# Three transpose groups a stretch instead of four, and the weight maximum moved to the head of the stretch

## The chip, the cores and the metric

The kernel runs on one core of a Trainium2 chip. The metric is device time in microseconds of one execution, compared with the kernel before on the same chip. The core has a matmul engine (TensorE, PE in the profile), a vector engine (VectorE, DVE), a scalar engine (ScalarE, ACT), a general engine (GpSimd, POOL) and a queue that issues transfers (SyncE, SP). Each works through its own instructions in order and waits for the others by semaphores. PE writes to PSUM, a small memory of eight banks; DVE and ACT read the results from there.

## What is computed

The reference is sigmoid attention, a Fourier mixing of its output, and a two-layer network, cut here to what matters:

```python
scores = scale * np.matmul(q, k.transpose(0, 1, 3, 2)) - np.log(S)
attn = 1.0 / (1.0 + np.exp(-scores))
x = np.matmul(attn, v)                    # (8, 12, 448, 64) -> (8, 448, 768)
mixed = np.real(np.fft.fft(np.fft.fft(x, axis=1), axis=2))
u = x + mixed
un = (u - mean(u)) / np.sqrt(var(u) + 1e-06)
out = u + np.maximum(un @ w_ch1, 0.0) @ w_ch2
```

There are 8 batches of 448 tokens, 12 heads of 64, a model width of 768 and a hidden width of 3072.

## The kernel before, in words

**Stages.** The program has three parts. In the first (0 to about 460 us of the profile) attention and mixing run for all eight batches. In the second, two blocks of 512 tokens go through the network with plain matmuls, while the weights are split into f16 pairs and stored. In the third (from about 950 us) the other five blocks use a fast product scheme; PE lines 790 and 841 are all of its chain.

**The attention loop.** The loop at line 518 takes two steps t, t+1 at a time; I call one pass a stretch and name it by its even t. There are 192 steps, 24 to a batch. In each stretch the code first empties three lists of work left over by the stretch before (`sp_next`, `act_next`, `dve_next`, lines 519 to 521: transfers, ACT copies, DVE additions). Then come two score blocks (`scores`, line 132: twelve matmuls on PE, two sigmoids on ACT, tile `a`), then two value blocks (`values`, line 152: eight matmuls on PE into `av`). Every second stretch, those with t a multiple of 4, finishes a head pair, and DVE copies `av` to `xT` (line 161). Then `mix_some` issues some mixing on PE. Last come the extras: POOL rounds q and k (`cast`, `qh` and `kh`, line 117), DVE makes the remainders (`rest`, `ql` and `kl`, line 122, also in the stretches with t a multiple of 4), POOL and DVE fold `xT` (`eo`, `fd`, `xp`, lines 175 to 181), loads are issued, and two more things happen: `weight_load` brings a piece of the weights (`wr`), and `weight_max` takes its largest magnitude on DVE (`wmax`, line 264). In the later batches DVE also computes the row statistics of finished tokens (`mv`, `un`, `hl`).

**The mixing.** One batch gives 36 units (lines 246 to 250), each with a cost in microseconds that the program's author wrote down: 24 of `stage_d` (0.33; one matmul each into `psd`), four of `stage_s` (0.65; `pss`) and eight of `add_x` (0.31). A unit of `add_x` is a group of three transposes on PE into one PSUM tile `psx` (line 226); the addition that reads the tile (`u`, line 233) goes to `dve_next`, so it stands on DVE at the head of the next stretch. `mix_some` gets a budget of `2 * UNIT_US` a stretch, adds it to what is left, and issues units while the balance is above zero; the last unit may overdraw it. All of `psd`, `pss` and `psx` share one pool of three PSUM tiles (line 91):

```python
ps_m = mix.enter_context(tc.tile_pool(name="ps_m", bufs=3, space=PSUM, side="right"))
```

A tile can be written again when its reader is done: ACT copies `A` (line 198) and `Q` (line 209), DVE operations `sm` and `df` (line 214), or the addition `u`.

**What fixes the order.** `pin()` at the end of each stretch ties every engine's instructions of that stretch to the order in which they were written. So an engine's order is that of the code, stretch after stretch.

**After the loop.** At step 170 `weight_scales` reduces the maxima (`wm`, DVE), has POOL reduce them over the partitions (line 272), and derives the scales; from there on weights are prepared (`prep_w`, lines 398 to 419: ACT, DVE, ACT, DVE). The last batch's units are issued after the loop by `mix_rest(0.65)` (line 616), together with pieces of the first network matmuls and weight steps.

Of the kernel before, what the change touches and what calls it, by code (L numbers as in the profile page):

```python
# [34 lines left out]
NW2 = 3  # L35
LEAD = 4
LNT = 2
UNIT_US = 0.57
MIX_UP = 8
MIX_STEP = 7  # L40

# [17 lines left out]
def spectral_attention_ffn(tc, q, k, v, w1, w2, cd, cs, ident_in, out):  # L59
# [8 lines left out]
    with ExitStack() as top:  # L68
# [19 lines left out]
        if True:  # L88
# [36 lines left out]
            def scores(t):  # L125

                g, c = divmod(t, 4)
                ps = ps_sc.tile([128, 2, 512], F32, tag="sc", name="sc")
                for n, (kn, qn) in enumerate(((0, 0), (0, 1), (1, 0))):
                    for j in range(2):  # L130
                        h = slice(j * D, (j + 1) * D)
                        nc.tensor.matmul(  # L132
                            ps[:CP, j, :SQ], split[g, 1, kn][h, c * CP:(c + 1) * CP], split[g, 0, qn][h],
                            start=(n == 0), stop=(n == 2))
                att[g, c] = a = wk.tile([CP, 2, SQ], F32, tag="a", name="a", bufs=ABUF)
                nc.scalar.activation(  # L136
                    a, ps[:CP, :, :SQ], AF.Sigmoid, bias=-math.log(S), scale=1.0 / math.sqrt(D))
# [3 lines left out]
            def values(t):  # L141
                g, c = divmod(t, 4)
                gg, pr = divmod(g, 2)
                b, r = divmod(gg, NG)
                p = r + 3 * pr
                a, vr = att.pop((g, c)), vrs[gg]
                if c == 0:
                    avp[g] = ps_av.tile([128, 512], F32, tag="av", name="av")
                ps = avp[g]
                for j in range(2):  # L150
                    h = 2 * pr + j
                    nc.tensor.matmul(  # L152
                        ps[j * D:(j + 1) * D, :SQ], vr[:, c, h * D:(h + 1) * D], a[:, j],
                        start=(c == 0), stop=(c == 3))
                if c < 3:
                    return
                if r == 0 and pr == 0:
                    xts[b] = (fx.tile([128, 6, 2, HS], F32, tag="xT", name="xT", bufs=2),
                              fx.tile([128, 2, 2, 2, 3, HM], F32, tag="xp", name="xp"))
                xT = xts[b][0]  # L160
                nc.vector.tensor_scalar(  # L161
                    out=xT[:, p].rearrange("d r k -> d (r k)"), in0=ps[:, :SQ], scalar1=1.0, scalar2=None,
                    op0=ALU.mult)
# [20 lines left out]
            def mix_units(b):  # L184
                xT, xp = xts[b]
                A = fx.tile([HM, 2, 2, 386], F32, tag="A", name="A")
                ps_d, sd, ut = {}, {}, {}

                def stage_d(kp, c, par, p):
                    m = HM - kp  # L190
                    if par == 0 and p == 0:
                        ps_d[c, kp] = ps_m.tile([128, 512], F32, tag="m", name="psd")
                    ps = ps_d[c, kp]
                    nc.tensor.matmul(
                        ps[:HM, par * 193:par * 193 + 193], xp[:, kp ^ c, c, par, p],
                        cd_sb[:, c, par, p], start=(p == 0), stop=(p == 2))
                    if par == 1 and p == 2:
                        act_next.append(lambda: nc.scalar.activation(
                            A[:, kp, c].rearrange("s (i r) -> s r i", r=2),
                            ps[:HM, 0:386].rearrange("s (r i) -> s r i", r=2), AF.Copy))  # L200

                def stage_s(kp, c):
                    m = HM - kp
                    ps = ps_m.tile([128, 512], F32, tag="m", name="pss")
                    nc.tensor.matmul(
                        ps[:m, :385], cs_sb[:, kp, c, :m], A[:, kp, c, :385], start=True, stop=True)
                    if c == 1:
                        sd["Q", kp] = Q = fx.tile([128, 385], F32, tag="Q", name="Q", bufs=2)
                        act_next.append(lambda: nc.scalar.activation(Q[:m], ps[:m, :385], AF.Copy))
                    else:  # L210
                        Q = sd["Q", kp]
                        sd[kp] = [fx.tile([128, 385], F32, tag=n, name=n, bufs=2) for n in ("sm", "df")]
                        for o, op in zip(sd[kp], (ALU.add, ALU.subtract)):
                            dve_next.append(lambda o=o, op=op: nc.vector.tensor_tensor(
                                out=o[:m], in0=ps[:m, :385], in1=Q[:m], op=op))

                def add_x(kp, r, hf):

                    lo, hi = (1, HM - 1) if r and not kp else (0, HM - kp)
                    s, d = sd[kp]  # L220
                    if hf == 0:
                        ut[kp, r] = fx.tile([128, DM], F32, tag="u", name="u", bufs=3)
                    u = ut[kp, r]
                    ps = ps_m.tile([128, 512], F32, tag="m", name="psx")
                    for i in range(3):
                        nc.tensor.transpose(
                            ps[:HM - kp, i * 128:(i + 1) * 128], xT[:, hf * 3 + i, r, kp:HS:2], ident)
                    y = d if hf == r else s
                    m = HM - kp
                    ysl = y[:m, 384:0:-1] if hf else y[:m, 0:384]  # L230

                    def add():
                        nc.vector.tensor_tensor(
                            out=u[:m, hf * 384:hf * 384 + 384], in0=ps[:m, :384], in1=ysl, op=ALU.add)
                        if hf:
                            base = b * S + (0, 113, 225, 336)[2 * r + kp] - lo

                            cut = lo + (hi - lo) // 16 * 16
                            for i, j in ((lo, cut), (cut, hi)):
                                if i < j:  # L240
                                    sp_next.append(lambda i=i, j=j: nc.sync.dma_start(
                                        u_dram[base + i:base + j, :], u[i:j, :]))
                    dve_next.append(add)


                res = [(0.33, lambda kp=kp, c=c, par=par, p=p: stage_d(kp, c, par, p))
                       for kp in range(2) for c in (1, 0) for par in range(2) for p in range(3)]
                res += [(0.65, lambda kp=kp, c=c: stage_s(kp, c)) for kp in range(2) for c in (1, 0)]
                res += [(0.31, lambda kp=kp, r=r, hf=hf: add_x(kp, r, hf))
                        for kp in range(2) for r in range(2) for hf in range(2)]  # L250
                return res

# [9 lines left out]
            def weight_max(n):  # L262
                i, f = divmod(n, NFC)
                nc.vector.tensor_reduce(
                    out=wmax[:, i, f:f + 1], in_=wtile.pop(n)[:, :, 1].bitcast(F32), op=ALU.max, axis=AX.X,
                    apply_absolute_value=True)
# [170 lines left out]
            def flush(todo):  # L437
                now = list(todo)
                todo.clear()
                for fn in now:  # L440
                    fn()
# [38 lines left out]
            when_w = {}  # L480
# [37 lines left out]
            for t in range(0, TQ + LAG + 4, 2):  # L518
                flush(sp_next)
                flush(act_next)  # L520
                flush(dve_next)
                for i in range(t, t + 2):
                    if i < TQ:
                        scores(i)
                for i in range(t - LAG, t - LAG + 2):
                    if 0 <= i < TQ:
                        values(i)
                mix_some(2 * UNIT_US)
                for i in range(t, t + 2):
                    for fn in extra.pop(i, ()):  # L530
                        fn()
                    for n in when_w.get(i - 1, ()):
                        weight_load(n + 2)
                    for n in when_w.get(i, ()):
                        weight_max(n)
                pin()
            assert not extra, sorted(extra)
            att_ctx.close()
# [2 lines left out]
        with ExitStack() as fast, ExitStack() as st, ExitStack() as early:  # L541
# [73 lines left out]
            while units or act_next or dve_next or sp_next:  # L615
# [4 lines left out]
                n = step % MIX_STEP  # L620
# [274 lines left out]
            for c in range(NPLAIN + 1, NCK):  # L895
                t = (c - NPLAIN - 1) * NQ * NU
# [3 lines left out]
            for g in range(NGR):  # L900
                t = g * NU
# [81 lines left out]
```

## Time and profile before

| | us |
|---|---|
| median of 3 runs (lowest to highest) | 1801.37 (1796.43 to 1805.48) |
| the profiled execution: its time | 1796.9 |
| its span, first to last instruction | 1795.1 |
| PE busy in the span | 1671.5 (93%) |
| DVE busy | 1290.0 (72%) |
| ACT busy | 602.4 (34%) |
| POOL busy | 194.3 (11%) |
| mean granted PE clock | 0.977 |

The time is 1.8 us more than the span, for what lies around it. A row of the table of waits reads: engine, what it was about to do, its line, the engine and line that released it, total idle time in us, number of waits, the longest. A row of the timeline reads: start in us, length in us, engine, line, operation, output and inputs, shapes, how many instructions are merged in the row, and in brackets the idle time before it and what ended it. A row of the stretches' table reads: from and to, length, then busy time and number of instructions of PE, of the weight loads (PEld), of DVE, ACT and POOL, the granted clock, the share of the transfer engines in use, and GB/s.

### The profile page before, as it was taken

How to read it: one execution, taken by the hardware profiler on the slowest of the kernel's cores; microseconds unless marked ns; L12 is line 12 of the kernel's file. 1: busy time of each engine (PE TensorE's matmuls, PEld its weight loads, DVE VectorE, ACT ScalarE, POOL GpSimd, SP SyncE). 2: the span in 40 equal slices, each digit the busy share in tenths (PEclk: the TensorE clock that was granted, in tenths of full speed). 3: DMA queues.
4: the chain of work that ended last, by engine and by line, in shares of the span. 5: the costliest groups of instructions: out<-in, count | busy, mean ns of one | idle time of the engine just before them, and what ended most of it. 6: DMA issues, size and time to landing. Idle time of an engine off the chain costs nothing. (4 is left out here: it accounts for less than half of the span.)

```text
span 1795.1 us, 27673 instructions
## 1 busy us (share of the span) xinstructions
PE 1671.5 (93%) x10996; PEld 1070.2 (60%) x10996; DVE 1290.0 (72%) x2481; ACT 602.4 (34%) x767; POOL 194.3 (11%) x220
## 2 busy tenths in 40 slices
PE   8999999987878777999799999999999999999997
PEld 3555555543533333545357777777777777777774
DVE  3545577656777777467755888888888887888668
ACT  4444444434333333123232322333233323233221
POOL 4434444334000000000000000000000000000000
PEclk9999999998988999999999999999999999999999
DMA  7666767654666664587887466656475656566561
GB/s 234 209 213 211 237 208 240 212 177 118 225 211 211 211 211 140 192 307 278 302 288 271 186 247 234 238 214 242 175 277 206 237 199 254 215 229 241 216 227 59
DMA packets 109139, 394.95 MB, mean 220 GB/s; under 512 B 23521, under 2 KB 49362, under 8 KB 93522
## 3 DMA queue, kind: packets, MB, share of 16 engines
q1 hardware_dynamic: 109010, 393.19, 62.2%
q8 instruction: 86, 1.41, 0.3%
q14 instruction: 43, 0.35, 0.1%
HBM read 316.08 MB, written 73.92 MB: 217 GB/s over the span
## 5 line engine op out<-in xcount | busy, mean ns | idle before, releaser
L841 PE MATMUL pso<-ws,H 128*128 128x384 f16 x2520 | 422.6, 326 | 0.9 <-DVE H L796 0.8
L790 PE MATMUL psf<-ut,ws 128*128 128x256 f16 x3780 | 422.1, 273 | 1.1 <-DVE ur L600 1.1
L790 PEld LDWEIGHTS <-ws 128*128 128x128 f16 x3780 | 369.9, 98 | 50.3 <-issue 1.4
L841 PEld LDWEIGHTS <-H 128*128 128x128 f16 x2520 | 246.4, 98 | 155.8 <-DVE H L796 1.1
L136 ACT ACTIVATE a<-sc 112x900 f32<-112x900 f32 x192 | 166.6, 917 | 156.3 <-PE sc L132 156.1
L850 DVE TENSOR_TENSOR acc<-pso,acc 128x384 f32<-128x384 f32 x350 | 181.9, 550 | 19.0 <-PE pso L841 19.0
L579 PE MATMUL po<-w2h,hh 128*128 128x512 f16 (+1 forms) x384 | 133.7, 348 | 55.5 <-ACT hh L567 54.8
L152 PE MATMUL av<-a,vr 112*64 112x450 f32 x768 | 172.9, 573 | 3.7 <-DVE xT L161 3.7
L815 ACT ACTIVATE F<-F 128x1024 f32<-128x1024 f32 x60 | 63.5, 1058 | 332.0 <-DVE F L796 332.0
L796 DVE TENSOR_TENSOR H<-F,H 128x1024 f16<-128x1024 f32 x120 | 129.5, 1087 | 46.8 <-ACT H L825 46.8
L560 PE MATMUL psh<-ut,w1h 128*128 128x512 f16 x504 | 151.1, 382 | 5.0 <-DVE hl L568 5.0
L579 PEld LDWEIGHTS <-hh 128*128 128x128 f16 x768 | 77.5, 103 | 114.7 <-ACT hh L567 66.0
L579 PE MATMUL po<-w2h,hl 128*128 128x512 f16 (+1 forms) x384 | 132.9, 346 | 3.8 <-DVE hl L568 1.5
L796 DVE TENSOR_TENSOR F<-X,psf 128x256 f32<-128x256 f32 x240 | 98.0, 418 | 51.1 <-PE psf L790 48.1
L579 PE MATMUL po<-w2l,hh 128*128 128x512 f16 (+1 forms) x384 | 133.0, 346 | 0.0
L161 DVE TENSOR_SCALAR xT<-av 128x450 f32<-128x450 f32 x48 | 30.1, 626 | 141.8 <-PE av L152 141.8
L825 ACT ACTIVATE H<-F 128x1792 f16<-128x1792 f32 x60 | 101.8, 1697 | 89.0 <-DVE F L796 89.0
L796 DVE TENSOR_TENSOR F<-F 128x256 f32<-128x256 f32 x240 | 91.2, 421 | 17.7 <-ACT F L815 13.7
L568 DVE SCALAR_TENSOR_TENSOR hl<-psh,hh 128x512 f16<-128x512 f32 x48 | 33.2, 691 | 98.2 <-ACT hh L567 98.1
L132 PE MATMUL sc<-qh,kh 64*112 64x450 f32 x384 | 82.1, 423 | 19.7 <-ACT a L136 10.3
L152 PEld LDWEIGHTS av<-a,vr 112*64 112x64 f32 x768 | 47.8, 139 | 82.9 <-issue 68.3
L560 PE MATMUL psh<-ut,w1l 128*128 128x512 f16 x252 | 96.2, 382 | 0.0
(92 smaller groups left out, 1954.2 us busy)
## 6 DMA issues: line engine op xcount, KB each, us to landing
ws<-w_dram SPq DMA_DIRECT2D x120, 1344.0 KB, 5.9
wr<-w_in SPq DMA_DIRECT2D x80, 768.0 KB, 4.7
t_dram<-wt SPq DMA_DIRECT2D x48, 384.0 KB, 2.3
cb<-t_dram SPq DMA_DIRECT2D x24, 768.0 KB, 5.5
spare<-w_in SPq DMA_DIRECT2D x16, 768.0 KB, 4.6
qr<-q_in SPq DMA_DIRECT2D x48, 225.0 KB, 3.8
kr<-k_in SPq DMA_DIRECT2D x48, 224.0 KB, 3.5
vr<-v_in SPq DMA_DIRECT2D x24, 448.0 KB
```

The source lines that it names most:

```text
L132: nc.tensor.matmul(ps[:CP, j, :SQ], split[g, 1, kn][h, c * CP:(c + 1) * CP], split[g, 0, qn][h], start=(n == 0), stop=(n == 2))
L136: nc.scalar.activation(a, ps[:CP, :, :SQ], AF.Sigmoid, bias=-math.log(S), scale=1.0 / math.sqrt(D))
L152: nc.tensor.matmul(ps[j * D:(j + 1) * D, :SQ], vr[:, c, h * D:(h + 1) * D], a[:, j], start=(c == 0), stop=(c == 3))
L560: nc.tensor.matmul(hs[c, f], l[f][:, m], r[:, m], start=(m == n == 0), stop=(m == NCC - 1 and n == 2))
L568: nc.vector.scalar_tensor_tensor(out=hl, in0=ps, scalar=0.0, in1=hh, op0=ALU.max, op1=ALU.subtract)
L579: nc.tensor.matmul(po[n][:, at:at + hi - lo], l[:, cols], r[f][:, lo:hi], start=(f == 0 and m == 0 and at == 0), stop=(f == NFC - 1 and m ...
L790: nc.tensor.matmul(ps[:, :TH], w[:, x, a, m * 128:(m + 1) * 128], ut[y][:, b, m], start=(m == n == 0), stop=(m == n == 2))
L796: nc.vector.tensor_tensor(out=o, in0=x, in1=y, op=op)
L815: nc.scalar.activation(F[:, 0:4], F[:, 0:4], AF.Relu)
L825: nc.scalar.activation(hts[P][:, 0], F[:, 1:8], AF.Copy)
L841: nc.tensor.matmul(ps[:, :384], H[:, x, a, tp * 128:(tp + 1) * 128], w[:, y, b], start=(j == n == 0), stop=(j == 1 and n == 2))
L850: later(0, lambda: nc.vector.tensor_tensor(out=to, in0=ps[:, :384], in1=to, op=ALU.add))
```

## The change

The budget of a stretch rises from 1.14 to 1.20 us, the written cost of a transpose group from 0.31 to 0.42, and `weight_max` moves: what stood at the end of a stretch now stands at the head of the next one, behind the emptied lists and ahead of the scores.

```diff
-UNIT_US = 0.57
+UNIT_US = 0.6
...
-                res += [(0.31, lambda kp=kp, r=r, hf=hf: add_x(kp, r, hf))
+                res += [(0.42, lambda kp=kp, r=r, hf=hf: add_x(kp, r, hf))
                         for kp in range(2) for r in range(2) for hf in range(2)]
...
                 flush(dve_next)
+                for i in range(t - 2, t):
+                    for n in when_w.get(i, ()):
+                        weight_max(n)
                 for i in range(t, t + 2):
                     if i < TQ:
                         scores(i)
...
                     for n in when_w.get(i - 1, ()):
                         weight_load(n + 2)
-                    for n in when_w.get(i, ()):
-                        weight_max(n)
```

What this does to PE's order is seen at the end of the first batch's mixing. PE before, from the last two `pss` to the last transposes (scores left out; one `av` row stands for a stretch, and the x9 of `psx` are three groups of three):

```order
L152 MATMUL av<-a,vr 64x450 x4
L205 MATMUL pss<-A,cs_sb 112x385 x2
...
L152 MATMUL av<-a,vr 64x450 x4
L226 MATMUL psx<-ident,xT 113x128 x9
...
L152 MATMUL av<-a,vr 64x450 x4
L226 MATMUL psx<-ident,xT 113x128 x3
L226 MATMUL psx<-ident,xT 112x128 x9
...
L152 MATMUL av<-a,vr 64x450 x4
L226 MATMUL psx<-ident,xT 112x128 x3
```

These are stretches 44, 46, 48 and 50: two `pss`, then three groups, four groups, one group. The same four stretches of PE in the changed kernel:

```order
L152 MATMUL av<-a,vr 64x450 x4
L205 MATMUL pss<-A,cs_sb 112x385
L226 MATMUL psx<-ident,xT 113x128 x3
...
L152 MATMUL av<-a,vr 64x450 x4
L226 MATMUL psx<-ident,xT 113x128 x9
...
L152 MATMUL av<-a,vr 64x450 x4
L226 MATMUL psx<-ident,xT 112x128 x9
...
L152 MATMUL av<-a,vr 64x450 x4
L226 MATMUL psx<-ident,xT 112x128 x3
```

Now they hold one `pss` and one group, three groups, three groups, one group; one `pss` has moved from stretch 44 to 42. The units of `stage_d` come 8, 3, 4, 4, 3, 2 a stretch where they came 7, 4, 3, 4, 3, 3. The pattern is the same for each of the seven batches that mix inside the loop.

On DVE the same place, as a difference (- before, + the change; `u` are the additions that free the transposes' tiles):

```order
 L214 TENSOR_TENSOR df<-pss,Q 112x385
-L264 TENSOR_REDUCE wmax<-wr 128x1
 L233 TENSOR_TENSOR u<-psx,df 113x384
 L233 TENSOR_TENSOR u<-psx,sm 113x384 x2
-L161 TENSOR_SCALAR xT<-av 128x450
-L122 TENSOR_TENSOR ql<-qr,qh 128x450
-L122 TENSOR_TENSOR kl<-kr,kh 128x448
-L264 TENSOR_REDUCE wmax<-wr 128x1
 L233 TENSOR_TENSOR u<-psx,df 113x384
+L264 TENSOR_REDUCE wmax<-wr 128x1
```

The fourth addition now stands ahead of `xT`, `ql` and `kl` of stretch 48, and the maximum stands behind the additions instead of ahead of them. On SP the store of the rows whose addition moved up goes ahead of four loads of the same stretch (`vr`, `wr`, `kr`, `qr`). POOL's order is unchanged.

## The prediction

> **What bounds the kernel now.** I read the busy time by parts of the span first; the two that the edit acts in are attention up to the reduction of the maxima, and the end of attention:
>
> ```profile
> 0.00:380.00 380.00, 359.10 (x2185) 196.03 (x2187) 216.54 (x357) 172.25 (x215) 163.75 (x194) 0.99 0.69 221
> 380.00:462.00 82.00, 63.12 (x315) 33.01 (x312) 47.34 (x83) 27.56 (x36) 30.14 (x26) 0.85 0.40 118
> ```
>
> Up to 380 us PE is busy 359 of 380 us while DVE, ACT and POOL are near half. What is left of PE's time there is best read from the table of waits. Between 100 and 380 us, PE's whole table, and then the others' longest:
>
> ```profile
> PE psx L226 <- DVE u L233: 13.4, 6, 2.7
> PE sc L132 <- ACT a L136: 0.6, 1, 0.6
> ...
> ACT a L136 <- PE sc L132: 107.0, 55, 5.9
> DVE xT L161 <- PE av L152: 86.5, 30, 6.3
> ```
>
> In 280 us PE stops for two reasons only: six times for an addition that has to free a transpose tile, and once for a sigmoid. ACT and DVE wait for PE instead, again and again. So here PE is the bound, and an idle microsecond of PE is a microsecond of the program. One of the six, from the timeline of stretch 48:
>
> ```profile
> 100.47 1.25 PE L226 MATMUL psx<-ident,xT 128*113 128x128 f32 x9
> 100.59 0.63 DVE L161 TENSOR_SCALAR xT<-av 128x450 f32<-128x450 f32 x1 [2.25 <-PE av L152]
> 101.67 1.40 DVE L122 TENSOR_TENSOR kl<-kr,kh 128x448 fp32r<-128x448 f32 x1
> 102.99 0.94 DVE L264 TENSOR_REDUCE wmax<-wr 128x1 f32<-128x768 f32 x1
> 103.86 1.01 DVE L233 TENSOR_TENSOR u<-psx,df 113x384 f32<-113x384 f32 x2
> 104.45 0.59 PE L226 MATMUL psx<-ident,xT 128*112 128x128 f32 x3 [2.74 <-DVE u L233]
> 105.27 0.37 PE L132 MATMUL sc<-ql,kh 64*112 64x450 f32 x2
> 106.39 1.73 PE L152 MATMUL av<-a,vr 112*64 112x450 f32 x8
> 108.05 0.59 PE L226 MATMUL psx<-ident,xT 128*112 128x128 f32 x3
> ```
>
> Three groups run at 100.47; the fourth finds all three tiles of the pool taken. The first of them is freed by an addition that stands on DVE behind `xT`, `ql`, `kl` and here a weight maximum, so PE sits until 104.45. The other five waits:
>
> ```profile
> 158.81 0.59 PE L226 MATMUL psx<-ident,xT 128*112 128x128 f32 x3 [2.10 <-DVE u L233]
> 212.97 0.59 PE L226 MATMUL psx<-ident,xT 128*112 128x128 f32 x3 [1.88 <-DVE u L233]
> 268.77 0.59 PE L226 MATMUL psx<-ident,xT 128*112 128x128 f32 x3 [2.74 <-DVE u L233]
> 323.16 0.59 PE L226 MATMUL psx<-ident,xT 128*112 128x128 f32 x3 [2.10 <-DVE u L233]
> 377.30 0.59 PE L226 MATMUL psx<-ident,xT 128*112 128x128 f32 x3 [1.88 <-DVE u L233]
> ```
>
> They are longest (2.74) where the maximum stands last before the additions. The seventh batch mixes while no scores are left to run, and does not wait.
>
> **The change part by part.** *No fourth group.* The stretch that held four groups holds three, so the wait for the fourth goes, if the moved groups find free tiles. Each new place, by the rows of the first batch:
>
> ```profile
> 94.61 0.55 DVE L214 TENSOR_TENSOR df<-pss,Q 112x385 f32<-112x385 f32 x1
> 96.22 1.25 PE L226 MATMUL psx<-ident,xT 128*113 128x128 f32 x9
> ```
>
> In the stretch with the first three groups, the third now needs the tile of the one group issued a stretch earlier. Its addition follows `df`: 94.61 + 0.55 + 0.56 = 95.7. A group costs (1.25 - 0.59) / 2 = 0.33 us of PE by the x9 and x3 rows, and one more comes before, so PE asks at 96.22 + 3 x 0.33 = 97.2: 1.5 us to spare. In the next stretch the tiles were freed at the head, two microseconds before use. The last group needs the first addition behind `kl`: 101.67 + 1.40 + 0.56 = 103.6, and PE now arrives at 101.72 (the end of the x9 at 100.47) plus 3.08 (the next stretch's scores and values, 104.97 to 108.05) = 104.8: 1.2 us to spare. So nothing waits at its new place, and the first five waits are worth 2.74 + 2.10 + 1.88 + 2.74 + 2.10 = 11.56 us.
>
> *The sixth wait* is worth nothing, because the end of attention hangs on another chain:
>
> ```profile
> 374.29 0.63 DVE L161 TENSOR_SCALAR xT<-av 128x450 f32<-128x450 f32 x1 [2.25 <-PE av L152]
> 376.70 1.01 DVE L233 TENSOR_TENSOR u<-psx,df 113x384 f32<-113x384 f32 x2
> 379.10 0.19 DVE L270 TENSOR_REDUCE wm<-wmax 128x2 f32<-128x48 f32 x1
> 386.58 0.37 POOL L272 PARTITION_ALL_REDUCE ws<-wm  x1 [10.29 <-issue]
> 389.71 2.85 PE L152 MATMUL av<-a,vr 112*64 112x450 f32 x8 [3.75 <-DVE xT L161]
> 394.24 0.97 POOL L178 TENSOR_TENSOR fd<-eo 128x450 f32<-128x450 f32 x1 [7.30 <-issue]
> 395.93 2.56 PE L194 MATMUL psd<-cd_sb,xp 128*113 128x193 f32 x10 [2.00 <-DVE xp L181]
> ```
>
> DVE's work after `xT` (374.29, before the wait at 375.4) leads to `wm`, POOL's reduction, DVE's `xT` of stretch 172 and PE's values at 389.71. PE reaches that place earlier by 1.88 and waits longer by as much. Bounds: 0 to 1.88. The reduction starts 7.29 us after `wm` is done (379.29), as long as POOL's pause before `fd`, so I take the chain to start at `wm`. One addition fewer stands ahead of `wm`: 0.47 us (1.01 for two that overlap) gained; bounds 0 and 0.47.
>
> *The clock at that place.* After the 3.75 us wait eight value matmuls take 2.85 us; after the 2.74 us wait the next eight take 1.73 (106.39) and the scores ahead of them 0.37: only long waits slow PE, so removing the short ones gives their length and no more. The Trainium skill, "TensorE: Matmul & The Clock Gate", section "HAM oscillation — how this bites in real kernels", asks for no idle gaps over about 3.4 us. By that rule too the sum has no clock term, but the wait at 389.71, grown to 5.1 us, could not be worse than it is.
>
> *Units elsewhere.* Stretch 174 gets eight `psd` units instead of seven, behind the 395.93 wait. At the slow rate there a unit is 2.56 / 5 = 0.51 us; what follows (values, `xT`, DVE's weight steps, ACT's sigmoids, PE's next scores) hangs on it: 0.5 us lost; bounds 0 and 0.51. One `pss` leaves stretch 188 for 186, where PE idles anyway:
>
> ```profile
> 436.13 0.90 PE L205 MATMUL pss<-A,cs_sb 113*113 113x385 f32 x2
> 443.53 0.72 PE L132 MATMUL sc<-qh,kh 64*112 64x450 f32 x2 [6.50 <-ACT a L136]
> 448.76 1.55 PE L205 MATMUL pss<-A,cs_sb 113*112 113x385 f32 x4
> 441.72 0.50 ACT L198 ACTIVATE A<-psd 113x386 f32<-113x386 f32 x1
> ```
>
> It needs the copy `A` of 441.72 to free its tile (442.2), then half of 1.55 = 0.78 us, so it ends at 443.0, before the 443.53 at which the scores behind it go. PE saves 0.74 to 0.78 after 448.76; bounds: if the scores slip by its whole length, 0. I take 0.74.
>
> *The maximum at the head.* It costs 0.94 us wherever it stands. At the new place it is ahead of `xT`, for which DVE idles (2.25 us at 100.59); if that cover were gone, `xT` would come 0.94 us later, and it is not needed until PE's next values, some 2 us on. Gone from stretch 108 it lets DVE start `un` sooner:
>
> ```profile
> 238.91 0.95 DVE L264 TENSOR_REDUCE wmax<-wr 128x1 f32<-128x768 f32 x1
> 241.80 0.84 ACT L345 ACTIVATE hl<-un 128x768 f16<-128x768 f32 x1 [4.59 <-DVE un L323]
> 243.99 0.46 PE L132 MATMUL sc<-qh,kh 64*112 64x450 f32 x2 [0.60 <-ACT a L136]
> ```
>
> ACT's `hl` and the sigmoid behind it move up by 0.95, so the single 0.60 us wait of PE goes: 0.6 gained; bounds 0 and 0.6.
>
> *After the loop* a group of cost 0.42 makes 19 steps out of 18. DVE does the same work ahead of the last addition, and DVE, not PE, paces the weight preparation there; nothing, within some 1.0 us (two additions) either way, since the first `po` waits for that addition:
>
> ```profile
> 483.04 0.38 PE L579 MATMUL po<-w2h,hh 128*128 128x512 f16 x1 [0.74 <-DVE u L233]
> ```
>
> From there the plain and fast blocks start as much earlier as PE ends the loop.
>
> *Sum:* 11.56 + 0 + 0.47 - 0.5 + 0.74 + 0.6 = 12.9 us. The profiled 1796.9 becomes 1784.0. That execution lay 4.5 us under the median of the three runs, 1801.37, so against the median it is 1788.5. With every bound at its worse end 11.56 - 0.5 - 1.0 = 10.1, at its better end 13.44 + 0.47 + 0.78 + 0.6 + 1.0 = 16.3.
>
> **The rivals.** *The wait only moves (no change).* PE, 2 us earlier in each batch, could find something else late: the fold `xp` for the next `psd`, the casts. For it: PE had no wait there because it was late itself. Against it: DVE and ACT idle for PE 86.5 and 107.0 us in these 280 us, more than ten times the 13.4. Only the 0.47 and 0.74 of the other chain would stay: about 1800.
>
> *The third group still waits (half the gain).* The margins are 1.2 and 1.5 us, and a single `kl` takes 1.40 us: one more such operation on DVE ahead of the addition uses them up. If six batches lost 1 us at each of the two places, that is 12; I price the rival at one of the two, 6: 1801.4 - 12.9 + 6 = 1794.5. Against it: the order puts no operation there.
>
> *The stores block the loads (slower).* The store of the moved addition now stands on SP ahead of `vr`, `wr`, `kr`, `qr`:
>
> ```profile
> 103.10 0.35 SPq L106 DMA_DIRECT2D kr<-k_in  x1
> 109.54 0.56 POOL L117 TENSOR_SCALAR kh<-kr 128x448 fp32r<-128x448 f32 x1
> ```
>
> SP is held until that addition, at about 98.9 (two groups' additions after the 96.22 row's groups), is done; `kr` goes at 103.10. It decides only when the addition comes more than 4 us late, after 103.10, and the cast at 109.54 is pushed past PE's need. Then six batches lose, say, the 4.5 us that one late `kh` cost at the start:
>
> ```profile
> PEld sc L132 <- POOL kh L117: 10.7, 9, 4.5
> ```
>
> 6 x 4.5 = 27, less 12.9: 1815.5. Nothing in the rows is near this point.
>
> *The edit does not do what it says* is ruled out by the order: every batch in the loop has three groups at most.
>
> **How the numbers follow.** The forecast holds 0.68, "only moves" 0.14, "half" 0.13, "stores" 0.05. A measurement of this kernel tells about 0.5%, 9.0 us, from no change. The forecast of 12.9 with run medians uncertain by some 3 us (the three runs spread over 9) lies beyond that in nine cases of ten, "half" in two of ten: faster 0.64. Slower: the stores, and a little noise of "only moves", 0.06; the rest, 0.30, is the same. The likeliest case alone runs from 1785 (16.3) to 1791.5 (10.1), plus noise; to hold eight in ten the range is 1783 to 1798, which takes in "half".
>
> **What would show it.** The row of PE's transposes waiting for `u` between 100 and 380 us should be gone or under 1 us, the wait at 389.71 should be some 5 us long though earlier in time, and PE should begin the first `po` about 13 us earlier than at 483.04. I am wrong if PE's table of waits there has new rows that sum to more than 4 us, or if the loop ends earlier and the plain blocks do not follow.

## The result

The changed kernel took 1778.70 us (median of four runs, 1774.48 to 1782.58), the kernel before beside it 1798.90 us: a ratio of 0.9888, with a 95% interval of 0.9841 to 0.9935. The gain is 20 us where 12.9 were forecast. Two later repeats of the same pair gave 0.9918 (0.9897 to 0.9939) and 0.9902 (0.9884 to 0.9919); over all sixteen runs of the change the gain is about 17 us. The sign was right, and the size was forecast too small by 4 us or more.

The profiled execution of the changed kernel took 1780.22 us, its span 1778.3. In the changed file the lines from 536 on are numbered one higher; kernels of the experiments that have lines added shift likewise.

The stretches' table of the changed kernel, over the same two parts as before the change:

```profile
0.00:380.00 380.00, 366.91 (x2236) 200.91 (x2236) 221.82 (x368) 177.01 (x220) 169.14 (x197) 0.99 0.72 228
380.00:462.00 82.00, 66.59 (x330) 40.43 (x331) 55.38 (x88) 30.41 (x42) 28.58 (x24) 0.85 0.42 122
```

PE is busy 366.9 of the first 380 us where it was busy 359.1. Its five longest kinds of wait over the whole loop, 0 to 460 us, from the changed kernel's table:

```profile
PE sc L132 <- ACT a L136: 7.4, 2, 4.2
PE pss L205 <- ACT A L198: 6.2, 1, 6.2
PE av L152 <- DVE xT L161: 5.8, 1, 5.8
PE sc L132 <- DVE qh L117: 4.6, 1, 4.6
PE psd L194 <- DVE xp L181: 1.5, 1, 1.5
```

All six waits of the transposes for `u` are gone, and so is the 0.60 us wait for a sigmoid. Between 100 and 380 us one wait is left, the one for `xT`, 5.8 us long; it is the wait that stood at 389.71 before, and it now ends at 374.28. The moved groups in the timeline of the changed kernel:

```profile
94.71 1.24 PE L226 MATMUL psx<-ident,xT 128*113 128x128 f32 x9
98.97 1.25 PE L226 MATMUL psx<-ident,xT 128*112 128x128 f32 x9
101.49 0.54 DVE L233 TENSOR_TENSOR u<-psx,df 112x384 f32<-112x384 f32 x1
102.89 0.93 DVE L264 TENSOR_REDUCE wmax<-wr 128x1 f32<-128x768 f32 x1
103.22 0.59 PE L226 MATMUL psx<-ident,xT 128*112 128x128 f32 x3
```

The last group starts at 103.22, 1.2 us after the addition at 101.49 has freed its tile at 102.03. The forecast margin was 1.2 us. The end of attention, and the first `po` of the plain blocks:

```profile
363.58 0.19 DVE L270 TENSOR_REDUCE wm<-wmax 128x2 f32<-128x48 f32 x1
371.15 0.37 POOL L272 PARTITION_ALL_REDUCE ws<-wm  x1 [9.91 <-issue]
374.28 3.27 PE L152 MATMUL av<-a,vr 112*64 112x450 f32 x8 [5.84 <-DVE xT L161]
380.58 4.20 PE L194 MATMUL psd<-cd_sb,xp 128*113 128x193 f32 x12 [1.47 <-DVE xp L181]
470.14 0.38 PE L580 MATMUL po<-w2h,hh 128*128 128x512 f16 x1 [2.27 <-DVE u L233]
```

The first `po` moved from 483.04 to 470.14, so PE is 12.9 us ahead at the end of attention, and the plain blocks follow.

**Where the two profiled executions part.** Taking the same instruction in both traces, the changed kernel leads by 1.5 us at 81 us (no transpose group has run yet), by 15.05 at the `xT` of 374 us, by 13.2 at 417 us, by 13.0 through the plain blocks to 711 us, and by 16.8 from 958 us to the end. The transposes act from 81 to 374 us. There 13.5 us are gained: 11.56 of length of the five counted waits, 0.8 where the sigmoid wait was, and some 0.25 us more than its length at each removed wait. The first 1.5 us, the 2 us given back after 374 us and the 3.8 us gained after 711 us need another explanation.

### The profile page after: what moved, and what is told of

Same layout as the page of the kernel before. It is cut to its first block, busy times and chain, and to the rows that moved or that the text cites. A ratio compares the mean times of both kernels' runs of the same rounds, so it can differ in the third digit from the quotient of the medians.

```text
span 1778.3 us, 27691 instructions
## 1 busy us (share of the span) xinstructions
PE 1667.2 (94%) x10996; PEld 1070.8 (60%) x10996; DVE 1292.6 (73%) x2481; ACT 602.4 (34%) x767; POOL 197.7 (11%) x220
## 5 line engine op out<-in xcount | busy, mean ns | idle before, releaser
L132 PE MATMUL sc<-qh,kh 64*112 64x450 f32 x384 | 81.9, 423 | 12.9 <-ACT a L136 7.4
```

The costliest lines, as they stand in the source:

```text
L132: nc.tensor.matmul(ps[:CP, j, :SQ], split[g, 1, kn][h, c * CP:(c + 1) * CP], split[g, 0, qn][h], start=(n == 0), stop=(n == 2))
```

## Experiments

**The same two programs again.** Neither file has any edit. They say what one execution's numbers are worth.

> The kernel before once more, for what two executions of one program differ by. Theory A (the part of the gain beyond the six waits is chance of single executions: the first 55 us, where loads of q and k are late, and 780 to 900 us, where weights are combined from transfers): its profile differs from the first profile of the same kernel by 1 to 4 us in one of these two places and by under 0.3 us elsewhere; ratio 1.000 within 0.003. Theory B (the change itself moves these two places): the two profiles of the kernel before agree within 0.5 us in both places; ratio 1.000 within 0.003.

> The changed kernel once more. Theory A: with more runs the gain comes down to the waits and their refill, 13 to 15 us, ratio 0.9920 to 0.9930; its profile keeps the lead of about 13 us at the first po of the plain blocks, and the further 3.7 us at 780 to 900 us come out otherwise. Theory B: 17 to 20 us, ratio 0.989 to 0.9905, and again 1.9 us in the first 55 us and 3 to 4 us at 780 to 900 us.

> The whole change once more, beside the three-group rule alone. Theory: 0.9905 to 0.9925, a gain of 13.5 to 17 us, and 2.5 us or more behind the three-group rule alone; the first result of the change (20 us) held some 5 us of chance. Rival: the first result was right, 0.989 or less, level with the three-group rule.

The kernel before, against itself, gave 1.001 (0.9995 to 1.0025); the change 0.9918 and 0.9902, gains of 14.7 and 17.6 us. Two places vary whatever the kernel is. One is the start: at 81 us the profiled executions of these and the other kernels of this section without an added operation stand between 4.3 us ahead of the first profile and 2.1 us behind it. PE's waits for `kh` in the first 60 us, of the kernel before and of the changed kernel's first repeat:

```profile
PE sc L132 <- POOL kh L117: 1.5, 1, 1.5
```

```profile
PE sc L132 <- POOL kh L117: 3.6, 1, 3.6
```

The other is the stretch from 711 to 958 us, where the network blocks and the transfers of the combined weights overlap. The three executions of the changed kernel gained 3.7, lost 0.7 and gained 4.7 us there; the repeat of the kernel before gained 2.1 on its own first profile. These are executions of the same instructions, so I take about 5 of the first 16.8 us between the profiles for chance. Between 81 and 374 us the gain does not vary: each of the three profiled executions of the changed kernel gains 13.5 us there on the first profile of the kernel before.

The repeat of the kernel before showed something else: it was expected to stay within 0.3 us of the first profile outside the two places, and it lost 4.6 us between 81 and 374 us. In the profile on which the prediction rests, PE took 3.60 us from the start of each fourth group to the next group (104.45 to 108.05). In the repeat, after the same 2.74 us wait:

```profile
104.64 0.59 PE L226 MATMUL psx<-ident,xT 128*112 128x128 f32 x3 [2.74 <-DVE u L233]
105.79 0.58 PE L132 MATMUL sc<-qh,kl 64*112 64x450 f32 x2
107.42 2.46 PE L152 MATMUL av<-a,vr 112*64 112x450 f32 x8
109.81 0.59 PE L226 MATMUL psx<-ident,xT 128*112 128x128 f32 x3
```

The eight value matmuls take 2.46 us instead of 1.73, and the way to the next group 5.17. The stretches' table over these twelve microseconds, first of the profile before, then of its repeat:

```profile
104.00:116.00 12.00, 11.55 (x74) 6.46 (x75) 7.00 (x12) 5.19 (x6) 5.13 (x6) 1.00 0.71 247
```

```profile
104.00:116.00 12.00, 11.36 (x65) 5.84 (x66) 6.19 (x12) 5.20 (x6) 4.58 (x6) 0.86 0.67 241
```

The granted clock was 1.00 in one and 0.86 in the other, behind a wait of the same length. In the repeat four of the six waits were followed by such a slow stretch, each of 1.4 to 1.6 us, two of them behind waits of only 1.88 us; in the first profile none were. So the forecast rested on an execution in which the waits happened to cost their length alone.

**Which of these waits are followed by a slow clock.** The traces' own records of the granted clock settle this. The clock falls to half in whole steps: in each of the fourteen profiled executions all slow spells begin at whole multiples of 3.413 us from one another, to within 3 ns, and last one or more such steps. So each execution has a raster of 3.41 us, and the program lies differently on it each time. The third wait is 1.88 us long in both profiles of the kernel before (up to 212.97 in the first, up to 214.76 in the repeat). The stretches' tables, cut at the steps of the raster, first of the profile before, then of its repeat:

```profile
209.28:212.69 3.41, 1.81 (x13) 1.04 (x9) 2.72 (x4) 0.20 (x1) 1.29 (x1) 1.00 0.69 235
212.69:216.10 3.41, 3.13 (x23) 1.85 (x23) 3.41 (x7) 1.64 (x2) 0.98 (x1) 1.00 1.03 341
```

```profile
211.33:214.75 3.42, 1.55 (x11) 1.04 (x9) 3.00 (x5) 0.00 (x0) 1.29 (x1) 1.00 0.66 200
214.75:218.16 3.41, 3.40 (x17) 2.19 (x17) 3.35 (x6) 0.92 (x1) 0.98 (x1) 0.50 1.03 322
```

In the first profile 1.60 us of the wait fall into one step and 0.28 into the next, and the clock stays at 1.00. In the repeat 1.87 us fall into one step, and the next step runs at 0.50. Between 60 and 372 us the fourteen executions have 26 steps at full clock with 1.86 us or more of idle PE, and each is followed by a step at half clock; 1227 have 1.75 us or less, and none is. From 372 to 900 us the border is less sharp, between 1.8 and 2.0 us. So what counts is how much idle time falls into one step. A wait of 3.72 us or more puts 1.86 into one step wherever it falls, a shorter one only by chance. An estimate from these numbers, with the raster equally likely anywhere: somewhat under one half for a wait of 1.88 us and 0.7 for one of 2.74, in all about 2.9 slow ones of the first five waits of the kernel before.

**What a short wait costs.** If a wait also costs clock, longer waits must cost more than their length. The kernel before got one, or two, more reductions of 0.94 us on DVE in the stretches that hold four groups, ahead of the addition that PE waits for (their result is not used):

```diff
+                if t % 24 == 0 and 48 <= t <= 168:
+                    for _ in range(1):      # 2 in the second kernel
+                        nc.vector.tensor_reduce(out=spent, in_=cd_sb..., op=ALU.max, ...)
                 pin()
```

> The kernel before with one more DVE operation of 0.94 us at the end of each of the six stretches with four groups; it reads a constant table and its result is not used. The six waits become about 2.8 to 3.7 us. Theory E (a wait costs its length and, by chance and more often the longer it is, a stretch at a slow PE clock of about 1.5 us): five waits count, 4.7 us in length and some 1 to 3 us in clock: 5.5 to 8 us slower, ratio 1.003 to 1.0045. Rival F (only the length counts): 4.7 us, ratio 1.0026, and the granted clock between 60 and 380 us no lower than before.

> The same with two such operations: waits of 3.75 to 4.6 us. Theory E: all six are followed by a slow stretch; against the kernel before 9.4 us in length and about 5 us in clock (six slow stretches of 1.5 where the kernel before has two or three on the mean): 13 to 16 us slower, ratio 1.007 to 1.009. Rival F: 9.4 us, ratio 1.005.

With one, the ratio was 1.0060 (1.0043 to 1.0077), 10.8 us slower; with two, 1.0074 (1.0062 to 1.0086), 13.3 us slower. The first is more than either theory had for it (8 us at most), the second what theory E had. PE's five counted waits between 100 and 372 us, in the first kernel and in the second:

```profile
PE psx L227 <- DVE u L234: 15.9, 5, 3.6
```

```profile
PE psx L227 <- DVE u L234: 20.8, 5, 4.6
```

The kernel before has 11.56 us in these five waits. So their length grew by 4.3 and by 9.2 us, and length alone would give 1.0024 and 1.0051; both lie below the intervals. The stretches' table from 60 to 372 us shows the rest: the profile before, then the first and the second of these kernels:

```profile
60.00:372.00 312.00, 299.85 (x1833) 167.73 (x1833) 185.60 (x313) 140.05 (x178) 133.76 (x156) 1.00 0.68 218
```

```profile
60.00:372.00 312.00, 295.55 (x1752) 163.53 (x1750) 182.40 (x306) 135.45 (x172) 124.52 (x145) 0.96 0.65 209
```

```profile
60.00:372.00 312.00, 290.60 (x1726) 161.03 (x1722) 183.24 (x306) 133.52 (x168) 122.68 (x143) 0.96 0.64 204
```

All of the ten counted waits of the two, 2.74 to 4.59 us long, were followed by 4.9 to 6.3 us to the next group instead of 3.6. Four profiled executions have the six waits at 2.74 us or less: the profile before, its repeat, and two kernels told of below, the one with only the maximum moved and the one with only POOL's chain taken away. Behind the first five waits they had none, three, three and four slow stretches (none, four, three and four behind all six). That is 2.5 of five on the mean, at about 1.5 us each, 3.8 us in all. In the two kernels with added operations a wait followed by one slow step cost 1.3 to 1.6 us beside its length, and one followed by two, 2.2 to 2.7: over the five waits 9.8 us with one operation and 8.8 with two. That is 6.0 and 5.0 us more than the mean of 3.8. With the lengths it makes 10.3 and 14.2 us, against 10.8 and 13.3 measured, inside both intervals (7.7 to 13.9 and 11.2 to 15.5). So in this range a longer wait is more surely a slow one, and a slow one costs its length and 1.3 to 2.7 us.

**Which part of the change acts.** Three kernels take it apart. The first has the new budget and cost, with the maximum at its old place; the second only moves the maximum; the third reaches three, three and two groups with the old budget of 0.57 and a cost of 0.39, so that no other unit moves:

```diff
-UNIT_US = 0.57
+UNIT_US = 0.6
...
-                res += [(0.31, lambda kp=kp, r=r, hf=hf: add_x(kp, r, hf))
+                res += [(0.42, lambda kp=kp, r=r, hf=hf: add_x(kp, r, hf))
```

> The budget 0.60 and the group's cost 0.42, the maximum left at the end of the stretch. Theory A (the six waits are the fourth group's): PE's waits for u between 100 and 380 us gone (under 1 us in all), the 0.6 us wait for a sigmoid in stretch 110 stays, lead at the first po 11 to 13 us; ratio 0.992 to 0.994. Rival C (the move of the maximum carries half of it): waits of about 0.9 us stay in the batches where the maximum stands before the additions, lead 6 to 9 us, ratio 0.995 to 0.997.

```diff
                 flush(dve_next)
+                for i in range(t - 2, t):
+                    for n in when_w.get(i, ()):
+                        weight_max(n)
...
-                    for n in when_w.get(i, ()):
-                        weight_max(n)
```

> The maximum moved to the head of the stretch, the costs as before, so four groups in a stretch. Theory A: the six waits stay, but all at the 1.88 us of the batches without a maximum there, 11.3 us in all instead of 13.4; with the sigmoid's 0.6 a gain of 2 to 3 us, ratio 0.998 to 0.999. Theory B, if the maximum is what moved the first 55 us: 4 to 5 us, ratio 0.9975, with 1.9 us of lead by 55 us.

```diff
-                res += [(0.31, lambda kp=kp, r=r, hf=hf: add_x(kp, r, hf))
+                res += [(0.39, lambda kp=kp, r=r, hf=hf: add_x(kp, r, hf))
```

> The kernel before with the group's cost at 0.39 and nothing else: three groups, three groups, two groups in the stretches that held three, four, one; the units of stage_d and stage_s stay where they were, and so does the maximum. Theory A (the gain is the fourth group's wait and what follows from it): PE's waits for u between 100 and 380 us under 1 us in all, gain as with the whole change, 13 to 16 us, ratio 0.991 to 0.993; stretch 174 keeps seven units, so the lead lost between 389 and 411 us is smaller by about 0.5 us. Rival (the moved units matter): 3 us or more less gain than the whole change, ratio 0.9935 or higher.

> The three-group rule alone once more (three, three and two groups, no other unit moved, the maximum at its old place), beside the whole change on the same chip. Theory: the moved units of the whole change (the eighth psd unit of stretch 174, the pss of stretch 186) cost 3 us or more at the end of attention, so this stays ahead: 0.9875 to 0.9905, and at least 2.5 us under the whole change, with PE between 385 and 411 us giving back about 2 us of its lead here and about 4 us there. Rival: the lead of the first run was chance of the start and of the stretch from 780 to 900 us; then both come to the same ratio, 0.9905 to 0.992, within 2 us of each other.

Costs alone gave 0.9911 (0.9887 to 0.9935), beside 0.9918 for the whole change on the same chip: the moved maximum adds nothing that can be seen once no group waits. By itself it gave 0.9976 (0.9963 to 0.9990), a gain of 4.3 us. There all six waits are 1.88 us long; PE's row between 100 and 380 us of that kernel:

```profile
PE psx L226 <- DVE u L233: 9.4, 5, 1.9
```

That is 2.2 us less in the first five (11.56 before), and the 0.60 wait is gone; so the maximum lengthened four of the six waits, and the rest of the 4.3 us is chance or clock.

The third kernel gave 0.9889 (0.9876 to 0.9902) in its first session and 0.9901 (0.9885 to 0.9917) in its second, where the whole change beside it gave 0.9902. The first result looked like 3 to 5 us over the whole change; side by side the two ended 0.15 us apart. So the expected 2.5 us is not there in the time, and the rival, chance, held. The traces do show a smaller difference at one place, behind the wait for `xp` at the end of attention. Two matmuls of a row make one `psd` unit. The twelve matmuls there (six of the eight units) took 4.20 us in the first profile of the whole change (380.58, above). The same row in its third profiled execution, and then the ten matmuls (five of seven units) in the third kernel's second:

```profile
377.91 2.22 PE L194 MATMUL psd<-cd_sb,xp 128*113 128x193 f32 x12 [1.54 <-DVE xp L181]
```

```profile
381.19 1.89 PE L194 MATMUL psd<-cd_sb,xp 128*113 128x193 f32 x10 [0.70 <-DVE xp L181]
```

The same twelve take 4.20 us at a granted clock of 0.50 or 2.22 us at 1.00. From 374 us to the start of the plain blocks (498 us before) the four executions with the moved units went between losing 2.0 and gaining 1.3 us on the first profile, 0.4 lost on the mean; the two without gained 1.8 and 1.3.

**What the sixth wait hung on.** The prediction counted the sixth wait as nothing, because the end of attention waits for POOL's reduction chain. To test this the chain was taken off the path: the scales are derived four steps later, and the folds of the seventh batch and the casts that stood behind the reduction on POOL go to DVE. This was done to the changed kernel, to the kernel before, and to the third kernel above:

```diff
-                        e = nc.vector if r == 2 and n % 2 else nc.gpsimd
+                        e = nc.vector if r == 2 and (n % 2 or b == TP // 24 - 1) else nc.gpsimd
...
-                    at(4 * g - 4 + n, lambda g=g, fn=fn: (fn(g, 0), fn(g, 1)))
+                    at(4 * g - 4 + n, (lambda g=g: (cast(g, 0, nc.vector), cast(g, 1, nc.vector)))
+                       if n == 0 and 4 * g - 4 == TP + 2 else lambda g=g, fn=fn: (fn(g, 0), fn(g, 1)))
...
             at(TP, weight_scales)
+            at(TP + 4, weight_scales_2)
```

> The changed kernel with the chain at the reduction of the maxima taken off DVE's and PE's path: the scales are computed two stretches later, and the folds and casts of POOL that stand behind the reduction are done by DVE. Theory A (the sixth wait's gain was lost because PE then waits for that chain, and slows its clock there): the waits of 5.8 us for xT and 1.5 us for xp go, the lead at the next stretches grows by 6 to 10 us, ratio 0.986 to 0.989 against the kernel before. Rival D (DVE's weight steps behind it are the real bound of the end of attention): the waits for the sigmoids grow by as much, gain against the changed kernel under 2 us, ratio 0.991 or higher.

> The kernel before, with POOL's late chain taken away alone: the weights' scales are computed two stretches later, and the folds and casts that stood behind the reduction on POOL go to DVE; the six four-group stretches stay. Theory: PE's waits of 3.75 us for xT and 2.00 us for xp at 389 to 398 us go, with the slow clock behind them, while all six waits for u stay and the sixth now counts: 8 to 12 us gained, 0.9935 to 0.9955. Rival, that the chain is worth as much here as behind the changed kernel, 14 us or more: 0.9925 or less. If the chain is not what the end of attention hangs on in this kernel: 1.000.

> The three-group rule alone together with POOL's late chain taken away. Theory: the two add up, since the first shortens PE's work up to 380 us and the second removes waits behind it: 29 to 34 us gained, 0.981 to 0.984, no slower than the changed kernel with the chain taken away (0.984) and up to 3 us faster, since the moved units are not in it. Rival: without the wait behind the reduction PE is at full clock there and the moved units cost nothing; then the same as that kernel, 0.984 to 0.985.

The changed kernel without the chain gave 0.9840 (0.9827 to 0.9853), 1767.58 us: a gain of 28.8 us on the kernel before, more than expected. The changed kernel did not run in that session; by the ratios of its own three sessions, 0.9888 to 0.9918, the chain is worth 9 to 14 us there. The kernel before without it gave 0.9948 (0.9934 to 0.9961), 9.4 us, as expected. The third kernel without it gave 0.9833 (0.9818 to 0.9849), 1767.79 us: 11.9 us under the third kernel beside it. The stretches' table from 372 to 420 us shows why, first for the kernel before, then for it without the chain:

```profile
372.00:420.00 48.00, 36.98 (x195) 20.55 (x193) 25.93 (x60) 15.47 (x19) 14.10 (x14) 0.86 0.46 151
```

```profile
372.00:420.00 48.00, 40.48 (x238) 22.78 (x234) 35.00 (x77) 19.85 (x26) 13.24 (x14) 0.93 0.52 173
```

PE is busy 3.5 us longer in the same 48 us, at 0.93 of its clock instead of 0.86; against the first profile it stands 4.0 us behind at 374 us and 6.2 ahead at 417. The timeline of the same kernel shows what became of the chain and of the sixth wait:

```profile
380.53 0.59 PE L226 MATMUL psx<-ident,xT 128*112 128x128 f32 x3 [1.09 <-DVE u L233]
...
383.19 0.71 POOL L274 PARTITION_ALL_REDUCE ws<-wm  x1 [7.55 <-DVE wm L272]
...
390.79 2.55 PE L194 MATMUL psd<-cd_sb,xp 128*113 128x193 f32 x14
392.82 0.58 POOL L117 TENSOR_SCALAR qh<-qr 128x450 fp32r<-128x450 f32 x1 [8.92 <-issue]
```

The reduction now runs 0.14 us after `wm` (382.85 to 383.05), and POOL still stands idle for 8.92 us behind it, but PE no longer stops for that. The 3.75 and 2.00 us waits are gone, and fourteen `psd` matmuls, all seven units, run in 2.55 us. Without this cover the sixth wait, 1.09 us here, should count (no run takes it away alone), which fits the chain being worth 2.5 us more where no sixth wait stands; the two gains' intervals are some 2.5 us wide to each side, so that much is not shown. In the third kernel without the chain PE does not stop once between 100 and 372 us:

```profile
100.00:372.00 272.00, 272.00 (x1681) 151.78 (x1677) 179.61 (x309) 129.12 (x164) 118.18 (x136) 1.00 0.73 234
```

Both kernels with three groups and no chain, 29 and 30 us faster than the kernel before, beat the change. Which of the two is better these runs do not tell.

## Why the prediction was wrong in size, step by step

*"No fourth group"* was right. The first five waits went, the moved groups found free tiles with the margin forecast, and nothing new waits between 100 and 374 us. Its 11.56 us is the length of the waits in the traces. Each removed wait gave some 0.25 us more, five times about 1.2 us, that the step did not count: the lead of the changed kernel grows by about 3.0 us where a 2.74 us wait was.

*"The clock at that place"* is the step that failed: "only long waits slow PE, so removing the short ones gives their length and no more". It compared one 2.74 us wait with a 3.75 us wait, in one execution in which no short wait was followed by a slow stretch. In the three other executions with these waits, or shorter ones, three or four of the first five were: 2.5 on the mean of all four, worth 3.8 us. What decides is the idle time within one step of the raster, 1.86 us or more, which the length of a wait shows only in part. That all five waits stayed under it in the one execution that was read was luck. The rule of the Trainium skill that the step quoted ("TensorE: Matmul & The Clock Gate", section "HAM oscillation — how this bites in real kernels", no idle gaps over about 3.4 us) said the same as the step and does not hold here: waits of 1.88 us were followed by granted clocks under 1.0.

The term that failed is therefore the length of the waits taken for their whole price. With 1.2 for what they gave together beside their length and 3.8 for the clock, 11.56 becomes 16.6; with 0.8 of the sigmoid wait 17.4; less 0.4 at the tail, 17.0. That is what the sixteen runs say (about 17). The 3.8 is a mean of four executions, with an uncertainty of some 1.5 us.

*"The sixth wait is worth nothing"* was right, and the runs show why. The wait for `xT` grew from 3.75 to 5.84 us ("some 5 us" was said), by 2.1 us where the sixth wait had been 1.88. This 5.84 us row now stands between 100 and 380 us, so by its letter the forecast's sign of being wrong (new rows there of more than 4 us) was met; it is the old wait, moved forward. With the chain taken away neither the wait for `xT` nor the one for `xp` is left.

*"Units elsewhere"* and the earlier `wm`, together +0.7 us in the sum, were wrong in sign as far as four executions tell: with the moved units the tail went between -2.0 and +1.3 us, 0.4 lost on the mean. The eighth `psd` unit runs behind a wait, and its price hangs on when the clock comes back. The `pss` moved to stretch 186 waits 6.21 us for the copy `A`, as foreseen, and takes 1.62 us where 0.78 was reckoned, so the scores behind it slip by 0.3; even so, in the first pair of profiles the lead grows from 12.6 us (ACT's rows at 442) to 13.3 (PE's at 451), the 0.74 of the sum. What the sum missed lies ahead of it, at the slow clock. The earlier `wm` did act: the reduction starts 9.9 us after POOL's last operation in the four executions with the moved units, and 10.2 to 10.5 us after it in three with the old order. But the 7.3 us from `wm` to the reduction are no fixed delay that `wm` starts, as the prediction took them: with two added operations they are 4.65 us, and without the chain 0.14.

*"The maximum at the head"* was right for the changed kernel: 0.6 forecast, 0.8 found at that place in the pair of profiles, and nothing that can be told in the times.

*"After the loop"* was right within its bound of 1.0 us: no large wait came in, though the one for `u` ahead of the first `po` grew from 0.74 to 2.27 us, and PE's lead went from 13.3 us at 451 to 12.9 there. The first `po` came 12.9 us earlier, where "about 13" was forecast, and that is in part luck: 1.5 of the 12.9 stood there at 81 us already. From 81 us to the first `po` the three executions of the changed kernel gained 11.4, 14.7 and 13.4 us on the first profile of the kernel before, in which no slow step followed the short waits.

*The reference.* The forecast was 1788.5, against a median of 1801.37 from three runs. The medians of four sessions put the kernel before at 1797.1 to 1798.9. Of the 9.8 us between forecast and first result, some 3 are this, 4 the clock and what the waits gave beside their length, and the rest the chance of four runs: the repeats gave 1782.1 and 1779.6. The range ended at 1783 because its lower end was built from the bounds of the terms and a little noise; it had no room for one profiled execution being a lucky one at the very place on which the sum rests.

*The rivals.* "The wait only moves" and "the third group still waits" have no row in the table after: nothing else was late in place of the additions, and no group waited. "The stores block the loads" has none either: up to 380 us PE waits for no cast of a loaded tile behind the start.

## What to carry to other kernels

A wait of PE of two or three microseconds has two prices: its length and, in executions in which 1.86 us or more of it fall into one step of the 3.41 us raster, 1.3 us or more of slow clock behind it. So look at more than one execution before a wait is priced, or work out the chance from its length, and compare the time from the wait to the next like instruction. Removing such waits early in a loop pays in full, while the last one, ahead of a chain on other engines, pays nothing until that chain is moved. When several kernels differ by 3 us, run them side by side again before explaining it: here the whole difference was chance.

## What was not expected of the hardware

Waits as short as 1.88 us were followed by a slow clock in some executions and not in others, of the same program at the same place, by where they fell on the raster: in the repeat of the kernel before behind both waits of 1.88 us and both of 2.74, but not behind those of 2.10; in the kernel before without POOL's chain behind those of 2.74 and 2.10, but not behind that of 1.88. With 2.74 to 4.59 us it was behind all ten counted, which for the shortest of them was still partly chance.

The reduction over partitions costs 0.37 to 0.72 us of POOL's time, yet POOL stands still for 9.5 to 10.8 us ahead of it in the eleven executions with the chain in place, and for 6.7 to 7.4 us after it. The pause ahead is no fixed time counted from `wm`: it ends 7.4 us after `wm` in the changed kernel (363.77 to 371.15), but 4.65 us after it in the kernel with two added operations, where `wm` came later. In the three kernels without the chain POOL had been idle for 6.9 to 7.7 us when `wm` came, and the reduction ran 0.14 us later; the pause behind it was 8.9 to 10.8 us. What POOL does in these pauses the traces do not show. It is the pauses, not the operation, that the other work has to be arranged around.
